# Sparse attention and an ELU MoE layer on one core: one fixed order of all operations, PSUM banks given by hand, batch 1 in unused tiles, an fp32 start and zero matmuls ahead of the data

## The chip, the cores and the metric

One core of a Trainium2 chip. The metric is device time in microseconds (us) of one execution, median over several executions; lower is better. Each execution has a state; "fast" is the undisturbed one, and all comparisons here are between fast runs. The kernel before runs at 361.99 us (358.71 to 362.79, three runs).

## The reference, cut to what matters

```python
# q, k, v: 8 batches x 8 heads x 576 positions x 64, fp32
scores = q @ k^T / sqrt(64)
mask_local   = (rel >= 0) & (rel < 32)                       # heads 0 to 3
mask_strided = (rel >= 0) & (key % 32 == query % 32)         # heads 4 to 7
attn = softmax(where(mask, scores, -1e9)) @ v                # per batch and head
x = attn as [4608 tokens, 512]
h = x @ w_in                                                 # 512 -> 2048
g = where(h > 0, h, exp(min(h, 0)) - 1)                      # ELU
out = g @ w_out                                              # 2048 -> 512
```

Of the kernel before, what the change touches and what calls it, by code (L numbers as in the profile page):

```python
# [15 lines left out]
S = 576  # L16
D = 64
# [12 lines left out]

@with_exitstack
def kernel(
# [16 lines left out]
    NCH = n_tokens // CHUNK  # L49
# [3 lines left out]
    weights = ctx.enter_context(tc.tile_pool(name="weights", bufs=1))  # L53
    p_in = ctx.enter_context(tc.tile_pool(name="qkv", bufs=2))
    p_wk = ctx.enter_context(tc.tile_pool(name="work", bufs=3))
    p_nm = ctx.enter_context(tc.tile_pool(name="norm", bufs=2))
    p_g = ctx.enter_context(tc.tile_pool(name="g", bufs=2))
    p_s = ctx.enter_context(tc.tile_pool(name="ps_s", bufs=1, space=bass.MemoryType.PSUM))
    p_v = ctx.enter_context(tc.tile_pool(name="ps_v", bufs=1, space=bass.MemoryType.PSUM))
    p_h = ctx.enter_context(tc.tile_pool(name="ps_h", bufs=2, space=bass.MemoryType.PSUM))  # L60
    p_o = ctx.enter_context(tc.tile_pool(name="ps_o", bufs=2, space=bass.MemoryType.PSUM))

    ctx.enter_context(tc.manual_schedule())

    nc.scalar.preload_act_table_set("natural_log_exp_and_others")

# [4 lines left out]
    vs_raw = consts.tile([RS, HG * NS, D], BF16, tag="vs", name="vs")  # L71

    def load_runs(nm, src, b, h0):
        t = vs_raw.rearrange("p n d -> p (n d)") if nm == "vs" else raw[nm]
        nc.gpsimd.dma_start(  # L75
            out=t[0:RS].rearrange("p (h f) -> p h f", h=HG),
            in_=src[b, h0:h0 + HG].rearrange("h (p s) d -> p h (s d)", s=NS))
# [8 lines left out]
    def load_kloc(b):  # L86
        t = raw["kl"][:, 0:HG * LB * D].rearrange("p (y t x d) -> p y t x d", y=2, t=LB, x=2)
        for h in range(HG):
# [4 lines left out]

    vl_t = [consts.tile([128, (2 * HG * LB + 1) * D], BF16, tag=f"vl{i}", name=f"vl{i}")
            for i in range(2)]
    vs_p = consts.tile([RS, (2 * HG * NS + 1) * D], BF16, tag="vsp", name="vsp")

# [10 lines left out]
    def copy_vloc(b):  # L108
        t = blocks(vl_t[b % 2], HG * LB)
        nc.vector.tensor_copy(t[0:PRE, 1:], t[128 - PRE:128, 0:HG * LB - 1])  # L110

    load_runs("qs", q, 0, HG)
    load_runs("ks", k, 0, HG)

    identity = consts.tile([128, 128], BF16, tag="identity")
    nc.vector.memset(identity, 1.0)
    nc.gpsimd.affine_select(
        identity, identity, compare_op=ALU.is_equal, fill=0.0,
        base=0, pattern=[[1, 128]], channel_multiplier=-1,
    )  # L120
    ones = consts.tile([128, D], BF16, tag="ones")
    nc.vector.memset(ones, 1.0)

    load_runs("vs", v, 0, HG)
    load_runs("ql", q, 0, 0)
    load_runs("kl", k, 0, 0)

    dist = consts.tile([RS, RS], I32, tag="dist")
    nc.gpsimd.iota(dist, pattern=[[1, RS]], base=RS, channel_multiplier=-1)
    same = consts.tile([RS, RS], I32, tag="same")  # L130
    nc.vector.tensor_scalar(same, dist, scalar1=STRIDE // NS - 1, scalar2=None,
                            op0=ALU.bitwise_and)
    eq = consts.tile([RS, RS], BF16, tag="eq")
    nc.vector.tensor_scalar(eq, same, scalar1=0, scalar2=None, op0=ALU.is_equal)
    mask_s = consts.tile([RS, RS], BF16, tag="mask_s")
    nc.vector.scalar_tensor_tensor(mask_s, dist, float(RS), eq, op0=ALU.is_ge, op1=ALU.mult)

    load_vloc(0)


    mask_l = consts.tile([128, 2, NS, 3, LN], BF16, tag="mask_l")
    nc.vector.memset(mask_l, 1.0)
# [7 lines left out]
    nc.vector.memset(mask_l[0:PRE, 0, :, 0, :], 0.0)  # L150

    w_in_sb = weights.tile([128, KC, d_ff], BF16, tag="w_in_sb")
    w_out_sb = weights.tile([128, MC, d_model], BF16, tag="w_out_sb")
    w_in_v = moe_w_in.rearrange("(kc p) f -> p kc f", p=128)
    w_out_v = moe_w_out.rearrange("(mc p) f -> p mc f", p=128)
    xT = weights.tile([128, KC, n_tokens], BF16, tag="xT")

    for i in range(4):
        nc.gpsimd.dma_start(out=w_in_sb[:, :, i * 512:(i + 1) * 512],
                            in_=w_in_v[:, :, i * 512:(i + 1) * 512])  # L160



    KSW = 2 * NS * RP + 128 - RP
    KLW = PRE + 2 * S
    qT = {"s": consts.tile([128, 2 * NS * RP], BF16, tag="qTs", name="qTs"),
          "l": consts.tile([128, 2 * NS * RP], BF16, tag="qTl", name="qTl")}
    kT = {"s": consts.tile([128, KSW], BF16, tag="kTs", name="kTs"),
          "l": consts.tile([128, KLW], BF16, tag="kTl", name="kTl")}
    kp = {(c, z): consts.tile([128, kT[c].shape[1]], BF16, tag=f"kp{c}{z}", name=f"kp{c}{z}")  # L170
          for c in "sl" for z in range(2)}
    nc.vector.memset(kT["s"][:, 2 * NS * RS:], 0.0)
    nc.vector.memset(kT["l"][:, 0:PRE], 0.0)
    nc.vector.memset(blocks(vl_t[0], HG * LB)[0:PRE, 0, :], 0.0)

    def set_up_later():
        nc.vector.memset(blocks(vl_t[1], HG * LB)[0:PRE, 0, :], 0.0)
        for (c, z), t in kp.items():
            nc.gpsimd.memset(t[(1 - z) * D:(2 - z) * D, :], 0.0)
            if c == "s":  # L180
                nc.gpsimd.memset(t[z * D:(z + 1) * D, 2 * NS * RP:], 0.0)
            else:
                nc.gpsimd.memset(t[z * D:(z + 1) * D, 0:PRE], 0.0)
        for t, n in ((vl_t[0], HG * LB), (vl_t[1], HG * LB), (vs_p, HG * NS)):
            nc.gpsimd.memset(t[:, 0:2 * n * D].rearrange("p (n w d) -> p n w d", w=2, d=D)[:, :, 0, :], 1.0)
            nc.gpsimd.memset(t[:, 2 * n * D:], 1.0)

    def load_batch(b, c):
        if c == "s":
            load_runs("qs", q, b, HG)  # L190
            load_runs("ks", k, b, HG)
            load_runs("vs", v, b, HG)
        elif b < NPE:
            load_runs("ql", q, b, 0)
            load_runs("kl", k, b, 0)
            load_vloc(b)
        else:
            load_qloc(b)
            load_kloc(b)
            load_vloc(b)  # L200

    def fill_pad():
        for nm, x in (("qs", q), ("ks", k), ("ql", q)):
            nc.gpsimd.dma_start(
                out=raw[nm][RS:RP].rearrange("p (h f) -> p h f", h=HG),
                in_=x[0, 0:HG].rearrange("h (p s) d -> p h (s d)", s=NS)[0:RP - RS])

    def dma_T(c):
        n = HG * NS // 2
        nc.sync.dma_start_transpose(  # L210
            out=qT[c].rearrange("c (n p) -> c n p", p=RP), in_=raw["q" + c])
        if c == "s":
            nc.sync.dma_start_transpose(
                out=kT[c][:, 0:n * RP].rearrange("c (n p) -> c n p", p=RP), in_=raw["ks"])
        else:
            nc.sync.dma_start_transpose(
                out=kT[c][:, PRE:].rearrange("c (n p) -> c n p", p=LQ),
                in_=raw["kl"][:, 0:HG * LB * D])
        s_ = slice(0, n * RP) if c == "s" else slice(PRE, KLW)
        for z in range(2):  # L220
            r = slice(z * D, (z + 1) * D)
            nc.sync.dma_start(out=kp[c, z][r, s_], in_=kT[c][r, s_])


    class Pair:
        def __init__(self, b, c, y):
            self.b, self.c, self.y = b, c, y
            self.old = b < NPE
            self.str = c == "s"
            self.rp = RS if self.old else RP  # L230
            self.q0 = y * NS * self.rp
            self.k0 = y * NS * self.rp if self.str else y * S
# [4 lines left out]
    def piece_T(P):  # L237
        for nm in "qk":
            ps = p_h.tile([128, S], BF16, tag="h", name="tp") if P.b == 0 else (
                p_s.tile([128, 2 * S], BF16, tag="s", name="tp")[:, 0:S])  # L240
            src = raw[nm + P.c][0:RS].rearrange("p (h f) -> p h f", h=HG)
            for i in range(NS):
                if P.str:
                    x, sp = divmod(i, NS // 2)
                    in_ = src[:, P.head(x), 2 * sp * D:2 * (sp + 1) * D]
                    nc.tensor.transpose(ps[:, i * RS:(i + 1) * RS], in_, identity[0:RS, 0:RS])
                else:
                    for x in range(2):
                        nc.tensor.transpose(
                            ps[x * D:(x + 1) * D, i * RS:(i + 1) * RS],  # L250
                            src[:, P.head(x), i * D:(i + 1) * D], identity[0:RS, 0:RS])
            if nm == "q":
                nc.vector.tensor_copy(qT[P.c][:, P.q0:P.q0 + S], ps)
            elif P.str:
                nc.vector.tensor_copy(kT[P.c][:, P.k0:P.k0 + S], ps)
            else:
                nc.vector.tensor_copy(
                    kT[P.c][:, PRE + P.k0:PRE + P.k0 + S].rearrange("c (p s) -> c p s", s=NS),
                    ps.rearrange("c (s p) -> c p s", s=NS))
# [91 lines left out]
    def piece_O(P, u, pm):  # L351
        if P.old:
            piece_O_old(P, u, pm)
            return
# [198 lines left out]
```

## The kernel before: the parts that the change touches

Positions are loaded by their remainder modulo 8, so that a strided head becomes eight dense blocks of 72 positions (a block holds four of the 32 stride classes, 18 positions of each); a local head becomes blocks of 96 queries against 128 keys. The tokens are worked in 9 chunks of 512; the attention of batch b + 1 runs between the matmuls of chunk b. An attention piece is: scores (TensorE), exp (ScalarE), product with a 0/1 mask (VectorE), values and row sums (TensorE), ln and exp of minus that for the reciprocal (ScalarE), product into xT (VectorE). A chunk is 16 first-layer groups of four matmuls, each group followed by exp (ScalarE), a clamp and a maximum (VectorE), and 16 second-layer groups of four matmuls.

The results of TensorE land in PSUM, a memory that both kernels use as 8 banks of 512 fp32 columns. Before, pools hand the banks out: two tiles of two banks for the attention, and four single ones.

```python
p_s = ctx.enter_context(tc.tile_pool(name="ps_s", bufs=1, space=bass.MemoryType.PSUM))
p_v = ctx.enter_context(tc.tile_pool(name="ps_v", bufs=1, space=bass.MemoryType.PSUM))
p_h = ctx.enter_context(tc.tile_pool(name="ps_h", bufs=2, space=bass.MemoryType.PSUM))
p_o = ctx.enter_context(tc.tile_pool(name="ps_o", bufs=2, space=bass.MemoryType.PSUM))
# ...
sc = p_s.tile([128, 2, 512], F32, tag="s", name="sc")        # scores: two neighbouring banks
# ... eight or six matmuls into sc[:, 0] and sc[:, 1], then ONE exp over both:
nc.scalar.activation(e[0:R], sc[0:R, :, 0:W], ACT.Exp, scale=scale)
# ...
ov = p_v.tile([128, 2, 512], F32, tag="ov", name="ov")       # values and sums: likewise
```

The order of the instructions comes from loops (`for m in range(16): ...`). Batches 0 and 1 are transposed on TensorE; later ones by DMA, which also builds copies of the keys padded with zeros, `kps` (strided) and `kpl` (local). All casting loads go through GpSimd's queue, in order.

The softmax here doesn't subtract the row's maximum and nothing guards it: scores larger than these inputs give would overflow.

## Time and profile before

| | before |
|---|---|
| time, median | 361.99 us |
| span of the profiled run | 357.7 us |
| TensorE busy | 316.0 us, 88% |
| VectorE / ScalarE busy | 239.3 / 218.4 us |
| mean granted clock | 0.962 |

The prediction below shows the page's main lines. In the page's fifth part each line is a group of instructions with its busy time, the mean ns of one, and the idle time of its engine just before such instructions:

```profile
L461 PE MATMUL ops<-w_out_sb,g 128*128 128x512 bf16 x576 | 146.2, 381 | 1.0 <-DVE g L438 1.0
L429 PE MATMUL hps<-xT,w_in_sb 128*128 128x512 bf16 x544 | 144.8, 390 | 0.0
```

The large matmuls, which are most of the work, had practically no idle time before them: 1.0 and 0.0 us.

### The profile page before, as it was taken

To read this page: it belongs to the slowest core of one execution; us is meant where nothing else is said; L and a number is where in the kernel's file an instruction comes from. 1 tells how busy PE (TensorE), PEld (TensorE's weight loads), DVE (VectorE), ACT (ScalarE), POOL (GpSimd) and SP (SyncE) were. 2 spreads that over 40 slices of the span, in tenths; PEclk is the share of its full clock that TensorE was granted. 3 is DMA by queue.
4 is the path that set the end of the run, shared out by engine and by line. 5 is a ranking of instruction groups with operands and counts; after the bars stand their busy time and mean duration, and the time that the engine had idled before them with its cause. 6 is when DMAs were issued, how large, how long until landed. Compare 5 with 4: busy or idle time off the path is not lost.

```text
span 357.7 us, 6115 instructions
## 1 busy us (share of the span) xinstructions
PE 316.0 (88%) x2272; PEld 156.7 (44%) x2272; DVE 239.3 (67%) x451; ACT 218.4 (61%) x373; POOL 93.2 (26%) x125
## 2 busy tenths in 40 slices
PE   1755685849999999999999999999999999999995
PEld 1542232324444445445544454454444444444442
DVE  2663566744777887877778877777877766666610
ACT  1571344526887778787878777888787644433411
POOL 7647804717110361036105310710000000000000
PEclk9999766787999999999999999999999999999999
DMA  6999945999975999699999988993621110111122
GB/s 92 186 204 180 206 70 56 141 159 163 91 125 120 131 159 146 139 104 156 122 191 122 179 147 118 137 151 96 102 62 34 48 40 29 37 52 31 29 74 76
DMA packets 110286, 40.29 MB, mean 113 GB/s; under 512 B 91856, under 2 KB 104112, under 8 KB 110256
## 3 DMA queue, kind: packets, MB, share of 16 engines
q0 software_dynamic: 71760, 19.05, 53.5%
q1 hardware_dynamic: 38496, 20.85, 29.5%
q8 instruction: 18, 0.29, 0.4%
q14 instruction: 12, 0.10, 0.1%
HBM read 38.03 MB, written 9.44 MB: 133 GB/s over the span
## 4 chain that ended last, share of the span: by engine, by line
PE 57%; DVE 17%; ACT 10%; DMA 9%; POOL 3%; issue 2%; SPq 0%; POOLq 0%; ACTq 0%
PE ops L461 24%; PE hps L429 23%; ACT rc L379 5%; DMA ks<-in_k_dram 5%; DVE g L438 4%; ACT ln L377 4%; DVE xT L383 4%; DVE he L436 3%; PE ov L364 3%; PE ov L371 3%; DMA kTs<-ks 3%; PE sc L283 2%; PE hps_o L429 2%; DMA kps<-kTs 2%; DVE xT L387 1%
## 5 line engine op out<-in xcount | busy, mean ns | idle before, releaser
L461 PE MATMUL ops<-w_out_sb,g 128*128 128x512 bf16 x576 | 146.2, 381 | 1.0 <-DVE g L438 1.0
L429 PE MATMUL hps<-xT,w_in_sb 128*128 128x512 bf16 x544 | 144.8, 390 | 0.0
L434 ACT ACTIVATE he<-hps 128x512 f32<-128x512 f32 x136 | 81.4, 598 | 48.6 <-PE hps L429 46.4
L438 DVE TENSOR_TENSOR g<-he,hps 128x512 bf16<-128x512 bf16 x136 | 93.6, 688 | 5.2
L461 PEld LDWEIGHTS <-g 128*128 128x128 bf16 x576 | 56.6, 98 | 69.8 <-issue 2.4
L436 DVE TENSOR_SCALAR he<-he 128x512 bf16<-128x512 f32 x144 | 63.3, 440 | 30.7 <-ACT he L434 29.7
L429 PEld LDWEIGHTS <-w_in_sb 128*128 128x128 bf16 x576 | 51.1, 100 | 48.2 <-issue 6.7
L286 ACT ACTIVATE e<-sc 72x576 bf16<-72x576 f32 (+1 forms) x64 | 41.7, 651 | 19.1 <-PE sc L283 18.8
L377 ACT ACTIVATE ln<-ov 64x576 f32<-64x576 f32 x48 | 31.0, 646 | 32.9 <-PE ov L364 16.7
L379 ACT ACTIVATE rc<-ln 64x576 f32<-64x576 f32 x48 | 32.8, 683 | 1.5
L387 DVE TENSOR_TENSOR xT<-ov,rc 64x576 bf16<-64x576 f32 x24 | 18.1, 755 | 19.9 <-ACT rc L379 19.9
L383 DVE TENSOR_TENSOR xT<-ov,rc 64x576 bf16<-64x576 f32 x24 | 18.1, 755 | 19.1 <-ACT rc L379 17.3
L466 ACT COPY osb<-ops 128x512 f32<-128x512 f32 x36 | 20.9, 582 | 13.6 <-PE ops L461 13.6
L82 POOL DMA_DIRECT2D ql<-in_q_dram x24 | 19.9, 836 | 25.5 <-DMA qTl<-ql 23.7
L75 POOL DMA_DIRECT2D vs<-in_v_dram x8 | 5.7, 714 | 60.6 <-DVE vsp L519 43.6
L288 DVE TENSOR_TENSOR pm<-e,mask_s 72x576 bf16<-72x576 bf16 x32 | 14.4, 449 | 6.1 <-ACT e L286 6.0
L89 POOL DMA_DIRECT2D kl<-in_k_dram x24 | 18.3, 786 | 0.1
L75 POOL DMA_DIRECT2D qs<-in_q_dram x8 | 6.1, 768 | 38.6 <-DMA qTs<-qs 37.7
L364 PEld LDWEIGHTS <-vsp 72*128 72x128 bf16 x192 | 9.5, 99 | 13.8 <-issue 11.0
L294 DVE TENSOR_TENSOR pm<-e,mask_l 128x576 bf16<-128x576 bf16 x32 | 14.5, 452 | 0.3 <-ACT e L286 0.2
L364 PE MATMUL ov<-pm,vsp 72*128 72x72 bf16 x192 | 10.3, 198 | 4.4 <-DVE pm L288 4.1
L434 ACT ACTIVATE he<-hps_o 128x512 f32<-128x512 f32 x8 | 4.8, 597 | 14.1 <-PE hps_o L429 14.0
(83 smaller groups left out, 210.5 us busy)
## 6 DMA issues: line engine op xcount, KB each, us to landing
out_dram<-osb SPq DMA_DIRECT2D x32, 144.0 KB
qs<-in_q_dram POOLq DMA_DIRECT2D x8, 288.0 KB, 5.8
ks<-in_k_dram POOLq DMA_DIRECT2D x8, 288.0 KB, 8.1
vs<-in_v_dram POOLq DMA_DIRECT2D x8, 288.0 KB, 6.6
vl<-in_v_dram POOLq DMA_DIRECT2D x8, 288.0 KB, 7.4
w_in_sb<-in_moe_w_in_dram POOLq DMA_DIRECT2D x4, 512.0 KB, 11.0
w_out_sb<-in_moe_w_out_dram POOLq DMA_DIRECT2D x4, 512.0 KB, 15.1
kps<-kTs SPq DMA_DIRECT2D x12, 160.0 KB
```

Of the source, the lines that this page charges most:

```text
L286: nc.scalar.activation(e[0:R], sc[0:R, :, 0:W], ACT.Exp, scale=scale)
L364: nc.tensor.matmul(ov[:, x, j * RS:(j + 1) * RS], lhsT=vs_p[:, c0:c0 + 128], rhs=pm[0:RS, z, n0:n0 + RS], start=True, stop=True, skip_grou ...
L377: nc.scalar.activation(ln[ys], ov[os_, :, 0:W], ACT.Ln)
L379: nc.scalar.activation(rc[ys], ln[ys], ACT.Exp, scale=-1.0)
L383: nc.vector.tensor_mul(xs[:, :, u * W:(u + 1) * W], ov[ys, :, 0:W], rc[ys])
L387: nc.vector.tensor_mul(xs.rearrange(pat, s=NS)[:, :, :, u * n:(u + 1) * n], ov[ys, :, 0:W].rearrange(pat, s=NS), rc[ys].rearrange(pat, s=NS))
L429: nc.tensor.matmul(hps, lhsT=w_in_sb[:, cc, m * 128:(m + 1) * 128], rhs=xT[:, cc, nb * CHUNK:(nb + 1) * CHUNK], start=(c == 0), stop=(c == ...
L434: nc.scalar.activation(e, hps, ACT.Exp)
L436: nc.vector.tensor_scalar(e1, e, scalar1=1.0, scalar2=1.0, op0=ALU.min, op1=ALU.subtract)
L438: nc.vector.tensor_tensor(g[:, m, :], e1, hps, op=ALU.max)
L461: nc.tensor.matmul(ops, lhsT=g[:, m, kk * 128:(kk + 1) * 128], rhs=w_out_sb[:, m, :], start=(m == 0), stop=(m == MC - 1))
L466: nc.scalar.copy(o_sb, ops)
```

## The change

Its intent: take the order out of the hands of loops and pools. One list of 1339 tokens gives the order of everything; each token names its PSUM bank or banks. `S.4s0.0.16` is the scores of batch 4, strided pair 0, half 0, in banks 1 and 6; `L.3.0.5` the first-layer group of chunk 3, block 0, in bank 5; `Z` second-layer groups; `O` values; `e`, `m`, `n`, `r`, `x` the exp, mask, ln, reciprocal and write of a piece; `h`, `i`/`j`/`p`, `g` the exp, the clamp (VectorE, ScalarE, GpSimd) and the maximum of the ELU; `Ls`, `Ll` the strided and local loads of a batch, `Ts` its DMA transposes, `Ks` the padded copies, `W` VectorE's copy of the strided v; `w` zero matmuls; `K` the casts of the fp32 start, `T` with a batch a transpose on TensorE, `b` the second half of a first-layer group. Of the 144 clamps six move to GpSimd and eight to ScalarE. The core of the diff, with cuts:

```diff
-    p_s = ctx.enter_context(tc.tile_pool(name="ps_s", bufs=1, space=bass.MemoryType.PSUM))
-    ... (ps_v, ps_h, ps_o likewise)
+    p_ps = ctx.enter_context(tc.tile_pool(name="ps", bufs=1, space=bass.MemoryType.PSUM))
+    ps = p_ps.tile([128, 8, 512], F32, tag="ps", name="ps")
...
+    def banks(s):                       # two banks i < j, as one strided view
+        i, j = int(s[0]), int(s[1])
+        return ps[:, i:j + 1:j - i, 0:W]
...
+    raw1 = {nm: xT[0:RS, i, n_tokens - HG * NS * D:]        # batch 1: end of xT, and g[1]
+            for i, nm in enumerate(("qs", "ks", "ql", "kl"))}
+    raw1["vs"] = g[1][0:RS, 0:HG * NS * D // CHUNK, :].rearrange("p a b -> p (a b)")
+    stage = g[0][0:RS, 0:8, :].rearrange("p a b -> p (a b)").bitcast(F32)
...
+    for nm, x, eng in (("q", q, nc.sync), ("k", k, nc.sync)):   # first pair, uncast
+        eng.dma_start(out=stage[...], in_=x[0, HG:HG + 2]...)
...
+    def warm(bank, n):
+        for _ in range(int(n)):
+            nc.tensor.matmul(ps[:, int(bank), 0:128], lhsT=zero, rhs=zero, ...)
...
+    for tok in ORDER.split():
+        f, *a = tok.split(".")
+        run[f](*a)
```

## The prediction

> **What bounds the kernel now.** I read the page first (busy shares, slices, chain), then the timeline of TensorE alone in the first 80 us and in one steady stretch, then those of GpSimd and of the sync queue. The page, shares and slices:
>
> ```profile
> PE 316.0 (88%) x2272; PEld 156.7 (44%) x2272; DVE 239.3 (67%) x451; ACT 218.4 (61%) x373; POOL 93.2 (26%) x125
> PE   1755685849999999999999999999999999999995
> DMA  6999945999975999699999988993621110111122
> PE 57%; DVE 17%; ACT 10%; DMA 9%; POOL 3%; issue 2%; SPq 0%; POOLq 0%; ACTq 0%
> ```
>
> TensorE is full from slice 10 on (a slice is 8.9 us), and ragged in the nine before: two kernels in one, a start of 80 us and a dense part. The start, TensorE's timeline:
>
> ```profile
> 6.37 0.66 PE L246 MATMUL tp<-identity,qs 72*128 72x72 bf16 x8 [6.37 <-DMA qs<-in_q_dram]
> ...
> 30.21 0.66 PE L246 MATMUL tp<-identity,ks 72*128 72x72 bf16 x8 [1.86 <-DMA ks<-in_k_dram]
> 30.68 1.90 PE L429 MATMUL hps<-xT,w_in_sb 128*128 128x512 bf16 x4
> ...
> 57.45 0.31 PE L326 MATMUL ov<-pm,ones 128*64 128x288 bf16 x2 [1.47 <-DVE xT L344]
> ...
> 80.01 0.58 PE L283 MATMUL sc<-qTs,kps 128*128 128x72 bf16 x7 [1.88 <-DMA kps<-kTs]
> ```
>
> The first layer (hps) is held until 30.68 behind batch 1's transposes, which stand ahead of it in TensorE's order and wait for data. Four 512-column matmuls take 1.90 there. One chunk's first layer (64 matmuls) and one batch's attention fill the time from 30 to 76. The dense part begins at 80.39, when batch 2's padded keys (kps) land. In the dense part:
>
> ```profile
> 102.68 1.03 PE L461 MATMUL ops<-w_out_sb,g 128*128 128x512 bf16 x4
> 103.66 0.42 PE L371 MATMUL ov<-pm,vl 128*128 128x96 bf16 x6
> ...
> 120.99 0.42 PE L364 MATMUL ov<-pm,vsp 72*128 72x72 bf16 x8 [0.62 <-DVE pm L288]
> ```
>
> Four matmuls take 0.8645 from start to start (99.84 to 100.70 and so on), so 0.216 each. A chunk with attention lasts 33.9 us (134.14 to 167.88 to 201.91 in the chain). Its 128 large matmuls are 27.7, leaving 6.2 for a batch. Sixteen attention groups at 0.256 (105.64 to 105.90) are 4.1; the other 2.1 are gaps ahead of the ov groups, where the mask product is not yet done (0.12 before 103.66, 0.80 before 120.99).
>
> Check of this reading: from 80.39 there remain 1152 - 64 - 4 = 1084 large matmuls, 234.3, and six batches at 6.2, 37.2: last matmul at 351.9. The trace has it at 353.55 (339.57 + 13.98). The rest, about 1.7, is the slow clock at 80 to 84. From there to the span's end are 4.1: a copy of 0.59 and the store.
>
> **What the Trainium skill says.** "TensorE: Matmul & The Clock Gate", Part 1: an idle array runs at half clock and is released after about 3.4 us of sustained work. The trace agrees: 1.89 for the four matmuls at 45.03 against 1.03 at 100.70, in a stretch with waits all through. "DMA: Bandwidth & Descriptors", section "SWDGE vs HWDGE vs iDMA": a transfer that casts has to be issued from GpSimd; that is why the change stages the first pair as fp32. Here GpSimd spends 0.7 to 0.9 us on each issue and the first cast load lands 5 us after its issue at 1.40; how fast an uncast one from the sync queue lands, no run yet shows. "SBUF — State Buffer", section "Who interferes with whom": VectorE's two-port modes and GpSimd lock each other out. The trace has a clamp (L436) of 0.79 at 33.25, beside GpSimd's memset of kps, against 0.43 usual; a few clamps on GpSimd are therefore no gift.
>
> **The change part by part.** Its instruction listing keeps the arithmetic: 144 first-layer groups and 144 second-layer groups of four matmuls, 64 score and 64 value groups.
>
> *Head.* q and k of the first pair come uncast over the sync queue, then 2 casts on VectorE (q) and 2 on ScalarE (k), some 0.5 each. First scores were at 10.18; I estimate 7 to 7.5. The 28 zero matmuls should have TensorE at full clock by then. Alone worth 3 us, but the weights decide what follows: the first w_in load is still issued near 10.3, and before it took 8.3 us to land.
>
> *First layer.* Chunk 0 no longer stands behind batch 1, so it starts at about 20 instead of 30.7. VectorE sets its pace: 12 clamps x 0.44 + 16 maxima x 0.69 = 16.3 us. Then batch 1 is interleaved with 11 second-layer groups. TensorE's work up to the first chunk-1 group is 64 x 0.216 + 7.4 (batch 1, from groups of 0.23 to 0.37) + 11 x 0.8645 = 30.7; VectorE's is 16.3 + about 11 for batch 1. From 21 that gives 52, with gaps about 54. The first scores of batch 2 come five groups later: TensorE wants them at 58.5.
>
> *Batch 2's data, the step that I think decides.* It goes through GpSimd's queue in order, then the sync queue:
>
> ```profile
> 24.02 0.79 POOL L478 DMA_DIRECT2D w_out_sb<-in_moe_w_out_dram  x1 [1.32 <-DMA w_in_sb<-in_moe_w_in_dram]
> 26.55 0.75 POOL L478 DMA_DIRECT2D w_out_sb<-in_moe_w_out_dram  x1 [1.74 <-DMA w_in_sb<-in_moe_w_in_dram]
> 27.93 0.74 POOL L478 DMA_DIRECT2D w_out_sb<-in_moe_w_out_dram  x1 [0.63 <-DMA qs<-in_q_dram]
> 30.45 0.74 POOL L478 DMA_DIRECT2D w_out_sb<-in_moe_w_out_dram  x1 [1.77 <-DMA ks<-in_k_dram]
> 31.23 1.20 POOL L179 MEMSET kps<- 64x1328 bf16 x1
> ...
> 41.55 0.42 POOL L186 MEMSET vsp<- 72x64 bf16 x1
> ...
> 56.98 0.56 POOL L204 DMA_DIRECT2D qs<-in_q_dram  x1
> ```
>
> Each issue from the ninth on waits for the load eight places ahead of it: the fill is paced by landings, one w_in quarter per 2.53 us. The listing has the same eight semaphores in turn. In the new order the last load (fourth quarter of w_out) waits for the second quarter of w_out, which the bytes ahead of it put at about 30. Then the memsets, 10.7 (31.23 to 41.97), so 41.5. Then ten local loads of batch 2 (8.0, as from 58.60 to 68.55 less waits): 49.5. Three strided loads and the pad rows: pad issued at 52. It lands 5.4 later (56.98 to the transpose at 62.43): 57.5. Then the sync queue:
>
> ```profile
> 62.43 1.40 SPq L210 DMA_TRANSPOSE qTs<-qs  x1
> 63.95 3.23 SPq L213 DMA_TRANSPOSE kTs<-ks  x1
> 73.02 1.18 SPq L222 DMA_DIRECT2D kps<-kTs  x2
> ```
>
> Transposes to the kps copy took 10.6 here beside loads, and 5.7 in the quieter turn at 99.53 to 105.23; I take 7. The copy then needed 4.9 to 7.0 (to 77.94 and 80.01); I take 5. Sum: 57.5 + 7 + 5 = 69.5, some 11 us after TensorE wants it. Before, it was 80.0.
>
> *Dense part.* After those scores stand 124 + 132 = 256 large groups, 221.3, and 96 attention groups at 0.256, 24.6: together 245.9. The value groups now stand further behind their masks, so the 2.1 per batch should mostly go; I leave 5 us of gaps in all. 69.5 + 245.9 + 5 = 320.4. The tail is as before, 4.1: span 324.5. The measured time is 1.7 above the span in the profiled run, 4.3 at the median of three: 327. This takes every term of the DMA chain at its likely value.
>
> **The rivals.** (a) The data comes in time: the order was laid so that the copy stands only five groups ahead of the scores. If GpSimd's fill runs without my waits, the scores run at 58.5 and the dense part ends at 309: span 313, time 316. For it: a tuned order presumably had some knowledge of these times. Against: the listing shows the semaphore waits. (b) VectorE or ScalarE binds. With attention VectorE has 26.8 us of work in a period of 33.9 and ScalarE 26.5; at my new period of 27.7 + 4.1 + 0.8 = 32.6 that is 82%, so gaps but no wall. But a clamp on GpSimd stands behind DMA issues that wait for transposes, and VectorE takes its work in order. If the gaps stay 2.1 per batch, +8: time 335. (c) TensorE stays cold in batch 0 and part of chunk 0: up to 64 x 0.216 = 14 us there, but hidden as long as batch 2's data is later; by itself it moves nothing. (d) The last three chunks lose their fine interleave: 16 first-layer groups in a row (0.8645 each) against VectorE's 1.13. With a bank cycle of seven, group 15 needs group 8's maximum, done at 9 x 1.13 + 1.3 = 11.5 while TensorE gets there at 13: no wait.
>
> **Range and chances.** I give (a) a third and the main line with some of (b) the rest: 316 and 327 weighted make 323. Eight in ten: 311 to 335, from a data chain that is on time and almost no gaps, to a chain at its slow values with the old gaps. Even the high end is 7% under 361.99; within 2% would need a cold or blocked dense part, which nothing in the listing suggests.
>
> **What would show it.** Right: TensorE idle some 6 to 12 us around 60 to 70, released by kps; GpSimd's memsets begin at 30 to 32; first scores at 7 to 8; chunk 0's first layer from about 20; attention periods of 32 to 33 with attention value groups following at once; 1.03 per four matmuls from about 25 on. Wrong: no such wait (then about 316); waits on VectorE's clamps or on a GpSimd clamp in each chunk (335 and above); the second wait, for batch 3's kps, as long as the first.

## The result, and the profile after

The changed kernel takes **404.76 us** (403.25 to 405.33, four fast runs) against 362.39 in the same rounds (358.71 to 363.16). The ratio is 1.1185, 95% interval 1.1103 to 1.1268: slower by 12%. (A ratio here and below is the mean time of one kernel's fast runs over the mean of the other's in the same rounds, so not quite the ratio of the medians.) The result is right, and the granted clock is the same, 0.961. The prediction was 323.

The same page of the changed kernel: shares, slices of TensorE, the chain of waits that ended last, and the two large groups.

```profile
PE 319.4 (79%) x2263; PEld 161.2 (40%) x2302; DVE 237.0 (59%) x431; ACT 228.0 (57%) x388; POOL 106.2 (26%) x135
PE   6896788675778777778577686878988789999995
...
PE 52%; DVE 18%; ACT 15%; DMA 8%; issue 4%; POOL 2%; SPq 0%; ACTq 0%; DVEq 0%; POOLq 0%
...
L629 PE MATMUL ps<-w_out_sb,g 128*128 128x512 bf16 x557 | 143.6, 390 | 20.5 <-DVE xT L547 8.6
L595 PE MATMUL ps<-xT,w_in_sb 128*128 128x512 bf16 x556 | 137.5, 383 | 16.5 <-DVE xT L547 6.3
```

TensorE and VectorE are busy for as long as before (within 3.4 us), ScalarE 10 and GpSimd 13 us longer. The start is better: slices 0 to 4 are fuller. But from there to slice 32 TensorE hardly gets to nine tenths; only the last chunks, which have no attention beside them, look as all of the dense part did before. And the large matmuls now have 20.5 and 16.5 us of idle time before them, of which the largest part ends with `DVE xT L547`, the write of an attention piece, an instruction of another stage. TensorE's longest sums of waits (us in total, times, longest):

```profile
PE ps L418 <- ACT ln L516: 9.5, 9, 2.0
PE ps L629 <- DVE xT L547: 8.6, 7, 2.1
PE ps L629 <- ACT e L425: 6.4, 9, 0.9
```

L418 are the scores, L629 the second layer, L595 the first. A second-layer group reads g and w_out; it has nothing to do with an attention exp, unless it wants that exp's bank. So the next step is to lay a stretch of the order beside the timeline. The tokens here are, with their banks and with cuts (`...` stands for tokens of the ELU and a reciprocal),

```
O.3l1.1.04 ... Z.2.0.1.2 ... n.3l1.1(0,4)  Z.2.0.2.2 ... S.4s0.0.16  x.3l1.1(0,4)  S.4s0.1.37  e.4s0.0(1,6)  Z.2.0.3.2
```

and the timeline of the changed kernel from the value group on (start, us, engine, operation, and in brackets the idle time before it and what ended it):

```profile
154.46 0.42 PE L488 MATMUL ps<-pm,vl 128*128 128x96 bf16 x6
154.72 1.02 PE L629 MATMUL ps<-w_out_sb,g 128*128 128x512 bf16 x4
...
155.78 0.64 ACT L516 ACTIVATE ln<-ps 64x576 f32<-64x576 f32 x1 [1.10 <-DVE he L612]
...
156.48 1.02 PE L629 MATMUL ps<-w_out_sb,g 128*128 128x512 bf16 x4 [0.73 <-ACT ln L516]
...
157.34 0.42 PE L418 MATMUL ps<-qTs,kps 128*128 128x72 bf16 x8
157.84 0.76 DVE L547 TENSOR_TENSOR xT<-ps,rc 64x576 bf16<-64x576 f32 x1 [1.33 <-PE ps L418]
158.65 0.42 PE L418 MATMUL ps<-qTs,kps 128*128 128x72 bf16 x8 [0.89 <-DVE xT L547]
...
159.77 1.02 PE L629 MATMUL ps<-w_out_sb,g 128*128 128x512 bf16 x4 [0.70 <-ACT e L425]
```

Read the banks into it. The second-layer group at 156.48 works in bank 2 and waits for a ln that reads banks 0 and 4. The write at 157.84 reads banks 0 and 4 and waits for scores that went to banks 1 and 6. The scores at 158.65, banks 3 and 7, wait for that write. The second-layer group at 159.77, bank 2, waits for an exp of banks 1 and 6. No pair of these shares a bank. In each of them one view's stretch of banks, from its lower to its upper, overlaps the other's. VectorE and ScalarE wait for TensorE in the same way, so the three engines, which should be running apart, are chained: 5.3 us from the value group to the third second-layer group.

The compiled program says the same thing without a timeline. It lists for each instruction the semaphore count it waits for, and so the instruction that it waits for. I counted the waits between TensorE, VectorE and ScalarE in which the two instructions share no tile and no bank, while their stretches of banks overlap: none in the kernel before, 187 in the changed kernel. (This counts the waits written into the instructions themselves; waits that stand ahead of one as an instruction of their own would come on top.) Of its 112 strided two-bank groups only 29 have neighbouring banks; the mean distance is 3.1. The "Trainium skill" page "PSUM — Partial Sum Buffer", section "PSUM bank collisions raise a hardware error", has as its rule to guard PSUM by bank and quadrant, "by bank is the simple version". These waits are coarser than that: they guard every bank that a strided view jumps over.

### The profile page after: what moved, and what is told of

It is laid out like the page before. It is cut to its first block, busy times and chain, and to the rows that moved or that the text cites. A ratio compares the mean times of both kernels' runs of the same rounds, so it can differ in the third digit from the quotient of the medians.

```text
span 403.4 us, 6126 instructions
## 1 busy us (share of the span) xinstructions
PE 319.4 (79%) x2263; PEld 161.2 (40%) x2302; DVE 237.0 (59%) x431; ACT 228.0 (57%) x388; POOL 106.2 (26%) x135
## 4 chain that ended last, share of the span: by engine, by line
PE 52%; DVE 18%; ACT 15%; DMA 8%; issue 4%; POOL 2%; SPq 0%; ACTq 0%; DVEq 0%; POOLq 0%
PE ps L629 24%; PE ps L595 21%; DVE xT L547 7%; ACT ln L516 6%; DVE g L623 5%; DVE he L612 5%; ACT e L425 4%; PE ps L418 4%; ACT he L603 2%; DMA kl<-in_k_dram 2%; ACT rc L522 2%; DMA kps<-kTs 2%; DMA qTs<-qs 2%; DMA ks<-in_k_dram 1%; PE ps L488 1%
## 5 line engine op out<-in xcount | busy, mean ns | idle before, releaser
L629 PE MATMUL ps<-w_out_sb,g 128*128 128x512 bf16 x557 | 143.6, 390 | 20.5 <-DVE xT L547 8.6
L595 PE MATMUL ps<-xT,w_in_sb 128*128 128x512 bf16 x556 | 137.5, 383 | 16.5 <-DVE xT L547 6.3
L603 ACT ACTIVATE he<-ps 128x512 f32<-128x512 f32 x144 | 84.4, 597 | 46.7 <-PE ps L595 36.0
L623 DVE TENSOR_TENSOR g<-he,ps 128x512 bf16<-128x512 bf16 x136 | 93.2, 687 | 21.7 <-ACT ln L516 7.3
L629 PEld LDWEIGHTS <-g 128*128 128x128 bf16 x576 | 54.4, 100 | 81.9 <-issue 30.7
L595 PEld LDWEIGHTS <-w_in_sb 128*128 128x128 bf16 x576 | 54.8, 98 | 79.7 <-issue 22.8
L547 DVE TENSOR_TENSOR xT<-ps,rc 64x576 bf16<-64x576 f32 (+1 forms) x64 | 43.4, 680 | 62.9 <-ACT e L425 15.8
L425 ACT ACTIVATE e<-ps 72x576 bf16<-72x576 f32 (+1 forms) x64 | 40.9, 647 | 33.5 <-PE ps L418 13.7
L516 ACT ACTIVATE ln<-ps 64x576 f32<-64x576 f32 (+1 forms) x64 | 37.4, 584 | 38.0 <-PE ps L629 10.7
L635 ACT COPY osb<-ps 128x512 f32<-128x512 f32 x36 | 21.1, 585 | 40.1 <-PE ps L629 36.5
L522 ACT ACTIVATE rc<-ln 64x576 f32<-64x576 f32 (+1 forms) x64 | 39.7, 621 | 2.0
L612 POOL TENSOR_SCALAR he<-he 128x512 bf16<-128x512 f32 x6 | 12.0, 2004 | 48.8 <-ACT he L603 48.8
L418 PE MATMUL ps<-qTs,kps 128*128 128x72 bf16 x192 | 10.6, 198 | 15.7 <-DVE xT L547 5.7
L418 PEld LDWEIGHTS <-kps 128*128 128x128 bf16 x192 | 9.1, 99 | 21.6 <-issue 18.8
L418 PE MATMUL ps<-qTl,kpl 128*128 128x96 bf16 x144 | 10.3, 211 | 5.4 <-ACT ln L516 4.1
```

The lines of the kernel that those rows point to most:

```text
L418: nc.tensor.matmul(dst, lhsT=kt[pr, k0:k0 + 128], rhs=rhs, start=True, stop=True, skip_group_check=True)
L425: nc.scalar.activation(e[0:R], tiles.pop(("S", key, u))[0:R], ACT.Exp, scale=scale)
L516: nc.scalar.activation(t, s_ps, ACT.Ln)
L522: nc.scalar.activation(t, tiles.pop(("ln", key, u)), ACT.Exp, scale=-1.0)
L547: nc.vector.tensor_mul(dst, o_ps, rc)
L595: nc.tensor.matmul(tiles["h", ch, m], lhsT=w_in_sb[:, c, m * 128:(m + 1) * 128], rhs=xT[:, c, ch * CHUNK:(ch + 1) * CHUNK], start=(c == 2) ...
```

## The experiments

**Theories.** A: the waits on banks in between are the loss. B (rival): the loss is in the order itself, that is, banks are reused too soon after their last reader, or the pieces stand too close to what they wait for; then bank numbers with the same reuse and no jumps change little. C (rival for what is left after A): the late data of batch 2, the clamps on GpSimd and the place of VectorE's work in the order. The runs were made on more than one chip, so they are compared by their ratios to the kernel before, which ran in the same rounds.

### Neighbouring banks, and banks far apart

Only the bank digits of the list change, by a new colouring of the same intervals of use: in the first every two-bank group gets neighbours, in the second its banks lie as far apart as can be. Order, engines and instructions are untouched. In the first the distance in the order from a bank's last use to its next stays about what it was (11 tokens on average in both).

```diff
-O.3l1.1.04 ... Z.2.0.1.2 ... n.3l1.1 Z.2.0.2.2 ... r.3l1.1 g.2.15 S.4s0.0.16 x.3l1.1 S.4s0.1.37   (changed kernel)
+O.3l1.1.67 ... Z.2.0.1.2 ... n.3l1.1 Z.2.0.2.2 ... r.3l1.1 g.2.15 S.4s0.0.45 x.3l1.1 S.4s0.1.01   (neighbours)
+O.3l1.1.07 ... Z.2.0.1.5 ... n.3l1.1 Z.2.0.2.5 ... r.3l1.1 g.2.15 S.4s0.0.16 x.3l1.1 S.4s0.1.07   (far)
```

> Only the bank numbers in the order differ from the changed kernel: every two-bank group sits in two neighbouring banks; same instructions, same sequence on every engine, same true reuse distances (mean 11 places). Theory A (a two-bank view with a stride is treated as holding every bank between its two, so instructions wait for readers and writers of banks they do not touch; the program of the changed kernel has 187 such waits, this one none): the dense part packs, the time falls to what I predicted for the change, 315 to 330 us. Rival B (the order itself is too tight: each engine meets its instructions in a fixed sequence, and small delays add up): stays within 3% of the changed kernel's 405 us. Rival C (late loads behind a clamp on GpSimd hold the engines): likewise about 395 to 405.

> Again only the bank numbers: pairs lie 6.1 banks apart in the mean (3.1 in the changed kernel, 1.0 in the run with neighbours), reuse distances alike; 335 of the waits name an instruction on a bank in between. Theory A: slower than the changed kernel, by the share of waits roughly, 420 to 520 us. Rivals B and C: 395 to 415, as nothing real changed.

Neighbours: **343.82 us** (341.72 to 345.21), ratio to the kernel before 0.9507 [0.9444, 0.9571]. Far: **503.4 us** (two runs, 500.26 and 506.53), ratio 1.3927 [1.3772, 1.4082]. Waits of the kind counted above: 0 and 335. So the same order runs at 344, 405 or 503 us when only bank numbers change. B falls. The far run shows the direction, but not a clean size: its page has a mean granted clock of 0.871 (0.961 in the changed kernel) and TensorE busy for 360.6 us against 319.4, so a third or more of its further 99 us is slower matmuls, and whether the idle stretches bring that clock is not shown. A few banks are also taken again sooner there, 31 of 444 within three tokens of the last use against 5 in the changed kernel. A's size was missed on one side: I expected 315 to 330 for the first, and 14 us more than that range remain, which is C's part. The same stretch with neighbours:

```profile
135.22 0.42 PE L487 MATMUL ps<-pm,vl 128*128 128x96 bf16 x6
...
135.48 1.89 PE L628 MATMUL ps<-w_out_sb,g 128*128 128x512 bf16 x8
135.68 0.64 ACT L515 ACTIVATE ln<-ps 64x576 f32<-64x576 f32 x1 [0.24 <-PE ps L487]
...
137.20 0.68 PE L417 MATMUL ps<-qTs,kps 128*128 128x72 bf16 x16
...
137.72 1.03 PE L628 MATMUL ps<-w_out_sb,g 128*128 128x512 bf16 x4
```

The two second-layer groups run in one go past the ln, both score groups in one go past the write, and from the value group to the third second-layer group it takes 2.5 us in place of 5.3. In the two pages, neighbours and then far, the large groups have this idle time:

```profile
L628 PE MATMUL ps<-w_out_sb,g 128*128 128x512 bf16 x576 | 142.4, 387 | 1.0 <-DVE g L622 0.9
L594 PE MATMUL ps<-xT,w_in_sb 128*128 128x512 bf16 x576 | 137.5, 381 | 1.4 <-DVE g L622 1.3
```

```profile
L594 PE MATMUL ps<-xT,w_in_sb 128*128 128x512 bf16 x576 | 157.3, 416 | 48.4 <-DVE xT L546 19.6
L628 PE MATMUL ps<-w_out_sb,g 128*128 128x512 bf16 x576 | 157.6, 413 | 37.8 <-DVE xT L546 19.3
```

1.0 and 1.4 us of idle time with neighbours, 20.5 and 16.5 in the changed kernel, 37.8 and 48.4 with far banks.

### The banks of the changed kernel, each two-bank instruction split in two

This keeps the bank numbers and takes away the strided views: exp, ln and write are issued once for each bank. If it is the views and not the numbers, the loss must go here too, though ScalarE and VectorE get more instructions.

```diff
-        return ps[:, i:j + 1:j - i, 0:W]
+        return [ps[:, b, 0:W] for b in (i, j)]
...
-        nc.scalar.activation(e[0:R], tiles.pop(("S", key, u))[0:R], ACT.Exp, scale=scale)
+        for z in range(2):
+            nc.scalar.activation(e[0:R, z], sc[z][0:R], ACT.Exp, scale=scale)
```

> The changed kernel with all its bank numbers kept; each two-bank exponential, logarithm and product is done as two one-bank instructions, so no instruction has a strided view over two banks (no wait names a bank in between). It costs per batch some 4 us more of ScalarE and 1.5 of VectorE (two of 0.41 in place of one of 0.65). Theory A: well under the changed kernel in spite of that, 345 to 370. If instead it is the spread of banks itself that slows the engines, or the order: 400 to 430.

**344.82 us** (343.95 to 344.93), ratio 0.9532 [0.9468, 0.9596]; no wait on a bank in between is left in the compiled program, and the idle time before the large groups is down to 1.4 and 2.2 us. This is just under the range that A expected: ScalarE has 500 instructions in place of 388, but is busy for only 230.7 us against 228.0 in the changed kernel, so the price was smaller than I had put it. The cause is settled: it is the strided view over two banks, with the waits that the program gives it, and either cure takes them away.

### The zero matmuls, and the fp32 start

Both on the version with neighbours: the first without the 30 zero matmuls, the second with the first pair over the casting queue of GpSimd as before, and no casts.

```diff
-w.2.28 K.q.1 ... w.4.1 ... w.2.1 ...        (e3: all w tokens out)
-K.q.1 K.q.0 K.k.1 K.k.0 ...                 (e4: K tokens and the staging loads out)
+    load_runs("qs", 0); load_runs("ks", 0)  # all four heads, casting
```

> The run with neighbouring banks, without the 30 zero matmuls. The trace of the changed kernel shows transposes of 0.66 us per eight right after them, no faster than cold, so I expect nothing: within 1% of the run with neighbouring banks. If the zero matmuls bring the clock forward, 2 to 5 us slower.

> The run with neighbouring banks, with the first pair of batch 0 loaded by the casting queue like the rest, without the four casts. First scores then start near 10 us instead of 8.7. If the head counts in full, 2 us slower; my view is that batch 2's keys or the weights decide the start, so 0 to 1 us slower.

**342.81** (0.9477 [0.9418, 0.9536]) and **341.98 us** (0.9504 [0.9413, 0.9595]), against 343.82 with both: no effect, as expected. In the changed kernel the zero matmuls ran from 1.05 to 4.22, and after a pause the first transposes still took this:

```profile
1.05 3.17 PE L363 MATMUL ps<-zero 128*128 128x128 bf16 x28 [1.05 <-DVE zero L289]
5.58 0.66 PE L382 MATMUL ps<-identity,qs 72*128 72x72 bf16 x8 [1.36 <-DVE qs L369]
```

0.66 us for eight is what they take without any zero matmuls, and what they took before; 30 us later such transposes take 0.42. But the zero matmuls do not always fail: in five of the twelve traces that show both (far banks, the casting queue, and e9, e12 and e13 below) the first eight took 0.43, in two of these (far banks and e13) the next three groups as well. In the run with the casting queue the next eight, 2 us on, took 0.66 again. The pauses do not sort the two kinds: 1.04 to 2.41 us before the fast ones, 1.04 to 1.36 before the slow ones. The fp32 start brings the first scores from 10.36 (casting queue) to 9.02, and nothing comes of it, since first-layer weights and batch 2's data decide what follows.

### What is left: GpSimd

In the version with neighbours, VectorE shows two long stops in the first 65 us:

```profile
36.58 5.02 DVE L611 TENSOR_SCALAR he<-he 128x512 bf16<-128x512 f32 x1
42.37 0.64 PE L381 MATMUL ps<-identity,xT 72*128 72x72 bf16 x8 [4.63 <-DVE g L622]
61.32 0.69 DVE L553 COPY vsp<-vs 72x2048 bf16<-72x2048 bf16 x1 [6.21 <-DMA vs<-in_v_dram]
62.79 0.45 PE L460 MATMUL ps<-pm,ones 128*64 128x288 bf16 x2 [5.67 <-DVE pm L437]
```

One clamp took 5.02 us in place of 0.42, while GpSimd ran memsets back to back (30.98 to 41.3), and TensorE stood 4.63 us behind it. And the copy `W.2` of batch 2's strided v stands in VectorE's order ahead of batch 1's last mask products, so TensorE waited 5.67 us for those. Two edits: the 14 later memsets put between the loads of GpSimd's queue; and the six GpSimd clamps (1.95 us each) given to VectorE; then both.

```diff
     for nm in LOADS:
         load(nm)
+        if nm in ("ks1", "vs1", "ql1", "kl1", "vl1", "wo2"):
+            fill(2)                     # two of the memsets
...
-p.1.2 ... p.1.6 ... p.2.6 ... p.2.8 ... p.3.12 ... p.3.13
+i.1.2 ... i.1.6 ... i.2.6 ... i.2.8 ... i.3.12 ... i.3.13
```

> The run with neighbouring banks; GpSimd's 14 later memsets (10.7 us) are put between the waits for landings in its load queue, instead of after them. Its queue is then free near 32 instead of 41.3, batch 2's loads, transposes and keys come some 8 us earlier, and TensorE's waits of 5.7 and 2.4 before batch 2's scores (and the 5 us clamp beside the memsets) should shrink: 330 to 337 if that chain is what remains of my miss. If it is not, no change (within 1% of 344).

> The run with neighbouring banks; the six clamps on GpSimd go to VectorE. Rival C (clamps behind DMA waits hold VectorE): 3 to 6 us faster. Otherwise within 1%.

> Both of the last two: the sum of their gains if they are separate, 326 to 335; my favourite for beating both kernels.

Memsets among the loads: **340.78 us** (0.9438 [0.9366, 0.951]), clamps on VectorE: **339.0** (0.9386 [0.9332, 0.9441]), both: **336.01** (three fast runs, 334.72 to 336.91; with the slow one the median is 336.46; 0.9293 [0.9226, 0.936]). The clamps give about 5 us, as the rival said. Both together give what the two give apart, and lie just above my 326 to 335. The memsets alone missed my 330 to 337, and their 3 us are not clear of the noise (the interval meets that of the version with neighbours): with them out of the way GpSimd's loads did not go earlier. Each waits for an earlier load to land, wo3 is reached at about the same time as with the memsets behind it, and batch 2's strided loads are still issued at 49.10 (49.47 before the edit) and the transposes start at 61.67 (61.62). The long clamp is gone from that trace, and the wait behind `W.2` grew to 6.8 us. The one stop had hidden the next. So it is the landings that pace this queue also at its end, where the prediction had put the memsets.

### VectorE's copy moved, then the strided loads first

On top of both: `W.2` 28 tokens later, and then `Ls.2` (strided loads of batch 2) in the place of `Ll.2` (local), which it swaps with.

```diff
-S.1l0.0.01 W.2 Ts.2 ... x.1l1.1 L.1.0.6 Ks.2 Ls.3
+S.1l0.0.01 Ts.2 ... x.1l1.1 L.1.0.6 Ks.2 W.2 Ls.3           (e9)
-h.0.11 Ll.2 b.0.13 ... e.1s1.0 Ls.2 T.1l1.q.4
+h.0.11 Ls.2 b.0.13 ... e.1s1.0 Ll.2 T.1l1.q.4               (e10, with e9)
```

> The previous version (neighbouring banks, no GpSimd clamps, memsets among the loads) with one token moved: the copy of batch 2's strided v on VectorE stands no longer ahead of batch 1's last products but 28 tokens later, just ahead of the next strided load. If late landing of batch 2's strided data sets the head (my theory): the 7.1 us wait of TensorE for pm goes, but the first scores of batch 2 then wait for kps instead, since the transposes start at 61.7 as before: time within 3 us of the previous version's 336.5, so 333 to 339. If the copy's place itself set the head (rival): 328 to 331.

> As the run before, and batch 2's strided loads issued ahead of its local loads (the two tokens swap places). My theory: the strided data land some 8 us sooner, the transposes start at 50 to 55 in place of 61.7, and the wait for kps at batch 2's first scores shrinks or goes: 325 to 330. Rival (the head is bound by the sum of work on TensorE, VectorE and ScalarE before batch 2): 333 to 337. Against it could stand the local data of batch 2 coming later, which would show as a wait for kpl or kTl near 90.

The copy alone: **338.34 us** (0.9359 [0.9292, 0.9426]), no gain. The strided loads first: **333.27** (three fast runs, 329.98 to 334.56; with the slow one the median is 333.92; 0.92 [0.9129, 0.9271]), faster than the version with the copy alone, as the two intervals do not meet. The waits of TensorE at batch 2's first scores, of e9 and then of e10 with the transfers ahead of it:

```profile
72.91 0.22 PE L422 MATMUL ps<-qTs,kps 128*128 128x72 bf16 x1 [10.13 <-DMA kps<-kTs]
```

```profile
54.06 0.75 SPq L651 DMA_DIRECT2D out_dram<-osb  x2
55.00 2.22 SPq L578 DMA_TRANSPOSE qTs<-qs  x1
...
65.10 1.19 SPq L592 DMA_DIRECT2D kps<-kTs  x2
...
70.28 0.19 PE L422 MATMUL ps<-qTs,kps 128*128 128x72 bf16 x1 [3.60 <-DMA kps<-kTs]
```

In e9 the wait moved from the mask products to kps, just as the theory of late data said: TensorE was ready at 62.8 and stood there for 10.1 us. In e10 the transposes start at 55.0 in place of 61.1, but from there to the scores it now takes 15.3 us in place of 11.8; the chain now runs beside the local loads that used to be ahead of it, but no run shows that this is why. Nor is 55.0 the landing: the transposes follow at once on a store of chunk 0 (54.06), which stands ahead of them in the sync queue and waits for ScalarE's copy of that chunk (53.45 to 54.03). The rows of q that they read had landed by about 51.8, an estimate from GpSimd's kl loads (four from 51.08 on), the second of which waits for the last of them. So part of what is left may be the place of that store in the order; no run moved it. And I missed my 325 to 330: of 6.1 us gained at the start of the transposes only 2.6 reach the first scores. The two profiled runs differ by 3.4 us (337.95 and 334.56), about these 2.6 and a wait for batch 3's kps that is 1.3 shorter; the fast medians differ by 5.1, and the rest I did not follow. This is the fastest version, 8% under the kernel before.

### Batch 1 in the tiles of batch 0

To value the unused tiles, the version with neighbours was given batch 1's loads in the same tiles as batch 0, with batch 2's loads after batch 1's last reads.

```diff
-        return (raw1 if b == 1 else raw)[nm]
+        return raw[nm]
   (cut: batch 1's loads, two w_out quarters and the memsets moved behind batch 0's last reads, Ll.2 and Ls.2 later)
```

> The version with neighbouring banks (343.8), with batch 1 loaded into the same tiles as batch 0 as in the kernel before; batch 2's loads stand after batch 1's last reads of them. My prediction put the arrival of data at the first layer and batch 2 as what this part buys: batch 1's loads then wait in GpSimd's queue for batch 0's transposes and values (until about 20), wo2 and wo3 behind them, and batch 2's strided loads wait for batch 1's last strided values (about 49): the transposes of batch 2 come at 66 or later in place of 61.7. Theory: 348 to 358. Rival (this part buys nothing, bandwidth limits the loads anyway): 341 to 346.

> The run before had batch 1's loads stand ahead of batch 0's reads in the program, so batch 0 computed with batch 1's data: its result was wrong and its time says nothing. Here the loads of batch 1, wo2, wo3 and the memsets are emitted after batch 0's last read of the shared tiles, else the same: the version with neighbouring banks (343.8) with batch 1 in the same tiles as batch 0. Theory (the unused regions buy an earlier start of batch 2's data): batch 2's transposes start at 66 or later in place of 61.7, time 348 to 358. Rival (the loads are limited by bandwidth anyway and this part buys nothing): 341 to 346. The result must be right.

> In the run before one last value group of batch 0 (O.0s0.1) still stood behind batch 1's load in the program: it waited 19.2 us for batch 1's v and the result was wrong. Here the loads stand behind it, else the same: the version with neighbouring banks (343.8) with batch 1 in the same tiles as batch 0. Theory (the unused regions buy an earlier start of batch 2's data): batch 2's transposes start at 66 or later in place of 61.7, time 348 to 358. Rival (the loads are limited by bandwidth anyway and this part buys nothing): 341 to 346. The result must be right.

The first two (e11, e12) were wrong kernels (relative error 0.46 and 0.23), and their times, 369.23 and 361.73 us, say nothing of the question: the loads of batch 1 stood in the program ahead of all, then of one, of batch 0's reads, which then waited for batch 1's data and used it. The third (e13) is right: **348.91 us** (347.72 to 350.83), ratio 0.9652 [0.9604, 0.97], so 5 us slower than the version with neighbours, at a granted clock of 0.933 to 0.957 in its four runs against 0.960 to 0.975 there. Batch 2's strided loads are issued at 57.05 in place of 49.47, its transposes start at 68.17 in place of 61.62 and its first scores at 80.62 in place of 73.86. The theory holds at the lower end of its range: the unused tiles, with the earlier places that they allow for the loads, are worth about 5 us here, of which the lower clock may be a part.

## Why the prediction was wrong, point by point

**The step that failed** is in the dense part and in rival (b): "The value groups now stand further behind their masks, so the 2.1 per batch should mostly go; I leave 5 us of gaps in all", and "82%, so gaps but no wall". I compared the two orders and the engines' sums, and took the banks given by hand for free: I never asked what a view with a stride of several banks would be made to wait for. In place of 5 us of gaps, the two large groups alone stood idle for 37.0 us in the changed kernel (20.5 and 16.5), 33.5 of it behind the exp, ln or write of an attention piece. The runs put a number on that: 404.8 with these banks, 343.8 with neighbours and 344.8 with split views, so **61 of the 82 us of the miss** (404.8 less 323). I could have seen it before any run, since the waits stand in the compiled program, 187 against none. What I did read there, the semaphores of the load queue, was the smaller matter.

**The terms of the sum**, read in the version with neighbours, where the in-between waits are gone:

- *First layer from about 20*: right, 20.39. *Memsets from 30 to 32*: right, 30.98. *Batch 2's pad issued at 52*: right, 51.63.
- *It lands 5.4 later, at 57.5*: too short. The transposes start at 61.62, 10 us after that issue. I had taken the landing time from the kernel before; here a local batch is in flight ahead of it (that this is the reason is argued, no run shows it alone).
- *7 and 5 to the scores, 69.5*: 5.2 and 7.0, right in sum. So the first scores come at 73.86 and 75.10: 4 to 6 us of the miss, 4.1 of it from the landing.
- *TensorE wants them at 58.5, some 11 us earlier*: 62.8 and a wait of 10.1 where nothing else stops it (e9). The picture of the main line was right, 4 us late at both ends. In the changed kernel itself two stops that I did not foresee, the clamp beside the memsets and the copy `W.2`, hid most of this wait.
- *Dense part 245.9 of work and 5 of gaps*: 251.1 busy and 9.0 idle from 75.10 to the last matmul at 335.2. The largest gaps are batch 3's wait for kps, 2.42 and 1.24 at 102 to 103, and 2.2 us of waits for maxima, which the version without GpSimd clamps does not have. I had named both as what would make it wrong, and both were small. Some of the 5 us of extra work may be slower matmuls ahead of the full clock; no run separates that.
- *Tail and outside the span*: 4.5 from the last matmul to the end of the span, predicted 4.1; the median lies 4.1 above the profiled span, where I had added 2.5.

Main line 327 against 343.8: about 6 us of it come from the first scores (75.1 for 69.5), and about 9 from the longer dense part (260.1 for 250.9), and 2 from the tail and what lies outside the span.

**The rivals.** (a), 316: wrong, the data was late in every version. (b): right in direction, and the mechanism was another one; no engine was near its limit. (c): hardly arose; in the version with neighbours 62 matmuls of chunk 0 took 14.62 us from 20.39 on, 0.236 each. (d): right, TensorE shows no wait from 240 us to its end there. **The head**: first scores came at 8.68, predicted 7 to 7.5, and the zero matmuls did not give the full clock to the first transposes of the changed kernel (in five other traces they did). The head was to be worth 3 us alone, but nothing while the data decides what follows, and it moved nothing.

**The chances**: eight in ten for 311 to 335, with even the high end 7% under the kernel before, was far too sure. It rested on "nothing in the listing suggests" a blocked dense part, and I had not looked at the part of the listing that did.

## What to carry to other kernels

When banks or buffers are given by hand inside one large tile, make every view one contiguous stretch: two banks taken with a stride can be guarded with all the banks between them, and engines that share nothing then run in turn. Look for it in the compiled waits, or in the profile as a large matmul that waits for an instruction of another stage; the test is to renumber the buffers and change nothing else. And when a stop is taken away, look for the next one behind it before counting its time as gained: here the clamp, the copy and the late transfers stood one behind the other, and each hid the next.

## What the Trainium skill lacked or had wrong

- "PSUM — Partial Sum Buffer": its rule is to guard by bank and quadrant. It does not say that a view over two banks with others between can come out guarded as one stretch. The guard here is a semaphore wait of the compiled program. 187 such waits cost 61 us (404.8 against 343.8), and with 335 of them the same order took 503.4.
- "TensorE: Matmul & The Clock Gate", Part 1: about 3.4 us of sustained work release the clock, and it warns that the moment varies from run to run. These runs agree: after 3.17 us of zero matmuls eight transposes took 0.43 us in five of twelve traces and 0.66 in seven. What they add is how soon it can be lost: in e4 the first eight took 0.43 and the next 0.66, with no pause longer than 2.41 us, and in e9 the third and fourth group slowed to 0.53 and 0.66 with none longer than 1.45.
- "SBUF — State Buffer", section "Who interferes with whom": it says that the one that comes second is blocked until the first one's instruction ends. In the version with neighbours a VectorE clamp lasted over a row of GpSimd memsets (36.61 to 41.31, three long and three short ones) and took 5.02 us, against 0.42 without. It stands with the same 5.02 in six of the traces with this row, the changed kernel's among them, each time starting 0.03 or 0.04 us ahead of the first long memset. But it is no rule: in the changed kernel's trace a clamp at 31.51, beside the earlier memsets, took 1.29 and ended while the row went on, and in the kernel before, beside the same row, none took over 0.79. Where loads stand between the memsets the longest is 2.65. When the waiting one gets its turn within such a row is not said.
- "DMA: Bandwidth & Descriptors": I found nothing in it that sizes a landing behind loads that are already in the queue. The same pad rows were followed by their transposes 5.4 us after the issue in the kernel before and 10 us after it here, with a local batch ahead of them.
